# First-norm row sums of two 256-row halves moved from VectorE to ScalarE, with a new instruction order

## The chip, the cores and the metric

One core of a Trainium2 chip runs the kernel. The metric is the device time in microseconds. "The kernel before" and "the changed kernel" are the two sides of the change.

Engines in the profile: PE is TensorE, DVE is VectorE, ACT is ScalarE, POOL is GpSimd, SP is SyncE, which here only issues DMAs. A line of a timeline holds the start in us, the duration in us, the engine, the source line, the operation, output<-input, the shape and the number of instructions in a row; in brackets stands how long the engine was idle just before and what ended that. SPq and ACTq lines are DMA issues.

## The reference

A transformer block in bf16 on x of 1 x 2048 x 512, conditioned on a vector c:

```python
mod = (silu(c) @ w_mod).reshape(1, 6, 1, 512)          # sa, ca, ga, sb, cb, gb
h = layernorm(x) * (1 + ca) + sa
x = x + ga * attention(h, wqkv, wo)    # 32 heads of 16, window of 8 keys, every second position
h = layernorm(x) * (1 + cb) + sb
x = x + gb * ((gelu(h @ w_gate) * (h @ w_up)) @ w_down)  # inner width 1792
```

## The kernel before

The 2048 rows are worked in five groups (g0, g1 of 256 rows, g2 to g4 of 512; a "half" is 256 rows). Python records 1016 operations with their reads and writes; a list `ORDER`, found by a search with a cost model, says in which order they are given out. The program gives each engine its own instructions in that order and sets semaphores between engines. Buffers are rings, used in the order in which their tiles first occur in `ORDER`.

```python
for tag, bufs in (..., ("xn1", 2), ("xn2", 2), ..., ("vR", 2), ("h2T", 2), ("gl", 3), ("ub", 3), ...):
    pool(tag, bufs)
for tag, bufs in (("psF", 4), ("psL", 2), ("psB", 2)):
    pool(tag, bufs, space=PSUM)
...
def ln(g, dst, off, p, seq, tags=("psF", "psF"), sums=None):
    for half in range(n // 256):
        ...
        if sums is not None:        # second norm: the sums came with the residual addition
            nm, var = sums[half], mv
            dve(... tensor_scalar_mul(out=nm[:], in0=nm[:], scalar1=-1.0 / D) ...)
            for i in range(2):
                act(... activation(out=xn[:, i, :], in_=x[g, c0 + i], func=ACT.Square,
                                   bias=nm[:, i:i + 1], accum_out=mv[:, 0, i:i + 1]) ...)
            dve(... rstd = mv / D + 1e-5 ...)
        else:                       # first norm
            for i in range(2):
                dve(... bn_stats(out=st[:, i, :], in_=x[g, c0 + i]) ...)
                dve(... bn_aggr(out=mv[:, i, :], in_=st[:, i, :]) ...)
            dve(... rstd = var + 1e-5 ...)
        gp(... rstd = rstd ** -0.5 ...)
        for i in range(2):
            dve(... xn = (x - mean) * rstd ...)
```

Attention's sums (over the features of each head, and later over the keys; "folds") are narrow matmuls: `tile_position=(0, 32 * d4)`, four 32-column tiles side by side (shape 128*32 in the profile); the others have the shape 128*128. v is written to DRAM (`scr`) and read back in copies that are shifted against each other (`vR`, four parts to a tile), half of them issued from SyncE's queue and half from ScalarE's. The rows of the first norm are transposed by TensorE for g0 to g2 and by a transposing DMA for g3 and g4 (`hT`), those of the second norm by a transposing DMA throughout (`h2T`).

Of the kernel before, what the change touches and what calls it, by code (L numbers as in the profile page):

```python
# [8 lines left out]
ACT = mybir.ActivationFunctionType  # L9
ALU = mybir.AluOpType  # L10
AX = mybir.AxisListType
F32 = mybir.dt.float32
# [6 lines left out]
    56, 7, 0, 55, 1, 4, 8, 9, 40, 42, 41, 33, 5, 6, 13, 137, 43, 16, 138, 44, 139, 10, 34, 45, 35, 36, 267, 140, 46,  # L19
    141, 273, 47, 142, 48, 11, 3, 51, 37, 38, 143, 39, 49, 274, 144, 148, 150, 50, 52, 265, 275, 276, 145, 146, 277,  # L20
    278, 53, 12, 57, 268, 266, 269, 54, 149, 279, 58, 270, 271, 28, 460, 59, 468, 461, 458, 2, 62, 147, 60, 61, 63,
    153, 14, 64, 272, 65, 154, 66, 459, 280, 466, 15, 70, 71, 32, 29, 462, 463, 18, 91, 67, 68, 69, 72, 90, 92, 93,
    467, 687, 281, 282, 283, 159, 160, 285, 284, 697, 161, 286, 288, 162, 17, 287, 94, 95, 96, 97, 98, 99, 469, 470,
    695, 151, 696, 163, 76, 164, 155, 74, 156, 157, 158, 297, 298, 471, 465, 100, 698, 152, 472, 101, 311, 312, 464,
    102, 103, 474, 77, 73, 75, 689, 170, 104, 78, 299, 85, 300, 303, 86, 304, 473, 105, 174, 313, 23, 314, 699, 79,
    173, 80, 305, 306, 690, 688, 172, 106, 691, 107, 108, 109, 293, 294, 309, 310, 291, 292, 171, 692, 110, 475, 476,
    478, 295, 20, 19, 301, 307, 81, 165, 21, 693, 111, 175, 112, 115, 176, 113, 117, 22, 116, 114, 694, 89, 290, 479,
    177, 700, 701, 118, 702, 289, 326, 24, 703, 477, 296, 328, 166, 302, 482, 498, 120, 168, 82, 83, 704, 25, 167,
    119, 123, 121, 124, 122, 308, 490, 178, 179, 481, 483, 169, 84, 180, 125, 499, 486, 127, 496, 491, 497, 494, 487,
    126, 327, 181, 484, 485, 495, 334, 182, 183, 492, 315, 333, 325, 493, 128, 335, 706, 336, 488, 500, 504, 184, 185,  # L30
    480, 329, 705, 708, 707, 129, 131, 330, 331, 332, 337, 501, 338, 339, 320, 340, 719, 130, 132, 489, 186, 341, 342,
    505, 187, 188, 727, 728, 720, 731, 732, 135, 502, 503, 136, 723, 733, 734, 729, 134, 133, 730, 316, 27, 26, 318,
    725, 724, 319, 189, 193, 343, 192, 196, 191, 190, 344, 194, 195, 197, 199, 345, 346, 347, 726, 721, 198, 717, 516,
    519, 722, 217, 219, 518, 227, 216, 520, 348, 317, 517, 718, 525, 349, 521, 522, 350, 351, 524, 526, 322, 523, 324,
    218, 226, 228, 221, 352, 229, 202, 222, 87, 88, 223, 710, 353, 354, 357, 220, 224, 241, 225, 200, 201, 203, 230,
    527, 243, 506, 247, 236, 249, 238, 246, 248, 242, 244, 232, 204, 205, 356, 355, 206, 207, 208, 245, 209, 250, 231,
    233, 234, 237, 715, 360, 361, 363, 239, 528, 529, 530, 358, 359, 716, 531, 533, 210, 321, 30, 31, 235, 323, 364,
    511, 512, 711, 712, 362, 240, 211, 215, 213, 214, 212, 713, 258, 709, 513, 259, 365, 366, 367, 260, 251, 261, 370,
    368, 747, 371, 369, 372, 373, 714, 748, 262, 755, 252, 253, 254, 255, 374, 375, 746, 408, 407, 409, 410, 376, 403,
    263, 405, 377, 382, 383, 418, 508, 420, 402, 404, 384, 515, 745, 256, 380, 514, 378, 381, 385, 386, 411, 379, 532,  # L40
    534, 387, 388, 389, 417, 419, 428, 430, 390, 391, 392, 406, 427, 429, 431, 535, 421, 413, 422, 412, 415, 414, 396,
    264, 507, 536, 257, 393, 394, 395, 432, 424, 416, 433, 435, 434, 754, 753, 537, 538, 423, 425, 444, 437, 438, 397,
    740, 749, 750, 751, 426, 752, 757, 758, 539, 540, 759, 541, 436, 542, 756, 509, 445, 439, 440, 446, 400, 510, 401,
    399, 441, 447, 448, 398, 648, 650, 543, 544, 649, 651, 557, 624, 623, 625, 626, 638, 598, 600, 442, 652, 546, 640,
    599, 659, 603, 639, 627, 545, 549, 550, 661, 558, 561, 760, 601, 605, 562, 564, 658, 553, 602, 660, 555, 455, 556,
    641, 642, 662, 452, 604, 606, 607, 613, 547, 762, 615, 548, 761, 619, 608, 610, 763, 621, 454, 614, 609, 559, 560,
    616, 551, 552, 554, 563, 451, 618, 620, 593, 611, 764, 765, 567, 612, 766, 622, 568, 735, 739, 767, 571, 617, 572,
    741, 736, 569, 633, 635, 595, 570, 580, 634, 565, 566, 743, 738, 453, 768, 769, 636, 582, 581, 573, 594, 596, 597,
    770, 637, 583, 771, 449, 457, 643, 645, 575, 450, 584, 586, 644, 653, 737, 646, 574, 576, 585, 456, 647, 655, 742,
    629, 631, 654, 772, 628, 630, 744, 656, 675, 577, 578, 663, 579, 632, 664, 773, 657, 775, 786, 785, 587, 443, 588,  # L50
    592, 591, 665, 666, 589, 676, 590, 681, 677, 678, 669, 774, 679, 680, 777, 776, 682, 683, 684, 685, 670, 671, 686,
    672, 667, 673, 778, 779, 780, 781, 787, 842, 782, 844, 838, 840, 783, 843, 845, 853, 852, 854, 837, 839, 784, 855,
    788, 790, 789, 792, 856, 791, 846, 793, 872, 832, 834, 794, 795, 796, 797, 857, 841, 874, 859, 858, 860, 833, 861,
    835, 836, 827, 829, 873, 888, 890, 875, 887, 800, 876, 802, 803, 804, 805, 806, 889, 828, 830, 831, 798, 847, 849,
    848, 891, 808, 850, 851, 823, 825, 867, 869, 822, 824, 799, 807, 826, 868, 870, 878, 883, 885, 882, 871, 801, 880,
    674, 668, 816, 809, 811, 810, 884, 886, 863, 877, 879, 865, 862, 864, 881, 866, 892, 812, 813, 814, 910, 911, 904,
    905, 815, 817, 893, 912, 898, 899, 913, 894, 906, 895, 900, 914, 896, 915, 907, 897, 908, 818, 820, 819, 821, 972,
    901, 902, 971, 974, 973, 976, 937, 978, 939, 936, 938, 975, 940, 927, 977, 979, 980, 929, 952, 954, 921, 923, 926,
    928, 922, 924, 925, 931, 951, 953, 955, 930, 933, 916, 941, 918, 943, 942, 944, 932, 934, 945, 935, 917, 919, 920,
    947, 949, 956, 957, 958, 959, 960, 961, 963, 962, 946, 982, 948, 964, 965, 981, 966, 950, 984, 967, 968, 969, 983,  # L60
    903, 909, 970, 986, 987, 988, 985, 989, 992, 993, 994, 995, 996, 997, 990, 991, 998, 999, 1000, 1001, 1004, 1005,
    1006, 1007, 1010, 1011, 1012, 1008, 1002, 1013, 1014, 1009, 1003, 1015,
# [153 lines left out]
def kernel(  # L216
# [13 lines left out]
    nc = tc.nc  # L230
    P = 128
    S, D = 2048, 512
# [9 lines left out]
    PLAIN = 2  # L242
    FIRST = (2, 0, 3, 1)

    pl = Plan(tc)
# [4 lines left out]
    for tag, bufs in (("xs", 4), ("wqkv", 3), ("woP", 1), ("Wg", 2), ("Wu", 2), ("WdP", 1), ("st", 3), ("mv", 4),  # L250
                      ("rstd", 4), ("xsum", 4), ("xn1", 2), ("xn2", 2), ("hT", 2), ("qT", 2), ("kT", 2), ("vT", 2), ("vR", 2), ("prod", 8),
                      ("Lb", 1), ("e", 1), ("rinv", 1), ("rhl", 1), ("oT", 1), ("h2T", 2), ("gl", 3),
                      ("ub", 3), ("hh", 15), ("ot", 2)):
        pool(tag, bufs)
# [10 lines left out]
    T = pl.tile  # L265
    E = Engines(nc, pl)
    pe, act, dve, gp, dma = E.pe, E.act, E.dve, E.pool, E.dma
# [102 lines left out]
    x = Rows()  # L370
# [31 lines left out]
    for b in (1, 0):  # L402
        dma(524e3, lambda dq, b=b: dq.dma_start(
            out=wm01[:, :, b * D:(b + 1) * D], in_=w_mod[:, b * D:(b + 1) * D].rearrange("(t p) n -> p t n", p=P)),
            w=[(wm01, b)], pri=-999.5 + 0.5 * (1 - b), bw=340e3)
# [6 lines left out]
    for d4 in range(4):  # L412
        dma(131e3, lambda dq, d4=d4: dq.dma_start(
            out=woP[32 * d4:32 * d4 + 32, :, :],
            in_=bass.AP(A_wo.tensor, A_wo.offset + 4 * D * d4, [[16 * D, H], [D, 4], [1, D]])), w=[(woP, d4)],
            pri=-987, bw=200e3)
# [77 lines left out]
    def ln(g, dst, off, p, seq, tags=("psF", "psF"), sums=None):  # L494
        n = GROUPS[g][1]
        xns = []
        for half in range(n // 256):
            c0 = 2 * half
            st = T("st", [P, 2, 6], F32, "st", seq)
# [4 lines left out]
            if sums is not None:  # L504
                nm, var = sums[half], mv
                dve(0.09, lambda nm=nm: nc.vector.tensor_scalar_mul(out=nm[:], in0=nm[:], scalar1=-1.0 / D), r=[nm],  # L506
                    w=[nm], pri=p)
# [17 lines left out]
            for i in range(2):  # L525
                def norm(i=i, xn=xn, mv=mv, rstd=rstd, c0=c0, nm=sums and sums[half]):
                    nc.vector.tensor_scalar(
                        out=xn[:, i, :], in0=x[g, c0 + i], scalar1=nm[:, i:i + 1] if nm else mv[:, i, 0:1],
                        scalar2=rstd[:, i:i + 1], op0=ALU.add if nm else ALU.subtract, op1=ALU.mult)

                dve(0.32, norm, r=[x.key(g, c0 + i), mv, rstd] + ([sums[half]] if sums else []), w=[(xn, i)], pri=p)
# [257 lines left out]
    def emit_ffn(g):  # L789
        n = GROUPS[g][1]  # L790
        nf = SG // n
        hh, ends = [], []
# [24 lines left out]
        for c4 in range(n // P):  # L817
# [4 lines left out]
            for part in range(parts):  # L822
# [3 lines left out]
                for lo, hi in ((0, 4), (4, 8), (8, 12), (12, 14)):  # L826
                    def down(lo=lo, hi=hi, c4=c4, y_ps=y_ps, c0=c0, w=w):
# [5 lines left out]
                       w=[y_ps], pri=p, after=ends if parts > 1 else ())  # L833
                ends.append(pl.ops[-1])
# [67 lines left out]
```

## Time and profile before

| | before |
|---|---|
| median of the runs | 243.25 us (242.82 to 243.60, 4 runs in all) |
| first q/k/v matmul | 12.56 us |
| end of the last y matmul | 238.23 us |
| between them, called "the stream" below | 225.67 us |
| ScalarE table loads | 7 |

The stream is what TensorE does without a real pause; what stands before it is the head. A kernel gets slower either because the head slips or because the stream gets longer, so I give both for every run. Each is read from the one execution that was profiled, so differences of a few tenths of a microsecond between two runs are not told from the scatter of executions unless a line of the trace shows where they lie. In the stream of before the profile records one wait of TensorE for another engine, 0.38 us for a gelu at 76.97 us.

### The profile page before, as it was taken

The page shows a single profiled execution, that of the slowest core. Times are in us where ns is not written, and L with a number is a line of the kernel's source. Part 1 is how long each engine was busy: PE and PEld are TensorE (multiplying, and loading weights), DVE is VectorE, ACT ScalarE, POOL GpSimd, SP SyncE. Part 2 cuts the span into 40 slices and gives each one's busy share as a digit, 9 for nine tenths or more (in the row PEclk, how much of TensorE's full clock was granted, in tenths as well). Part 3 has the DMA queues.
Part 4 walks back from the last instruction along what each step waited for, and adds up shares of the span by engine and source line. Part 5 has one row for each costly group of instructions (what it writes and reads, how often), then busy time and mean ns, then how long its engine had stood idle before and what let it go on. Part 6 is the DMA issues. An engine that isn't in the chain of part 4 may idle for free.

```text
span 241.7 us, 4320 instructions
## 1 busy us (share of the span) xinstructions
PE 234.1 (97%) x1664; PEld 128.3 (53%) x1681; DVE 164.1 (68%) x317; ACT 149.5 (62%) x278; POOL 23.3 (10%) x45
## 2 busy tenths in 40 slices
PE   7799999999999999999999999999999999999994
PEld 3499656545677546784444444444444444444443
DVE  4799999998998999775898878873425314131222
ACT  2179889699955763888458894426566542666300
POOL 5548030020000100110000001000010100000000
PEclk9999999999999999999999999999999999999999
DMA  5995899998999150369000837411002022000011
GB/s 178 355 337 159 175 244 307 188 301 209 348 289 252 48 133 3 88 146 210 1 3 0 164 60 175 87 45 44 3 0 45 0 46 87 0 0 0 3 43 43
DMA packets 38970, 29.10 MB, mean 120 GB/s; under 512 B 14117, under 2 KB 38054, under 8 KB 38950
## 3 DMA queue, kind: packets, MB, share of 16 engines
q1 hardware_dynamic: 33424, 24.55, 40.1%
q10 hardware_dynamic: 5526, 4.28, 7.6%
q8 instruction: 13, 0.21, 0.4%
q14 instruction: 7, 0.06, 0.1%
HBM read 21.40 MB, written 4.28 MB: 106 GB/s over the span
## 4 chain that ended last, share of the span: by engine, by line
PE 84%; DVE 6%; DMA 5%; issue 1%; ACT 1%; SPq 0%; POOL 0%; ACTq 0%
PE y_ps L829 20%; PE u_ps L802 18%; PE qkv_ps L604 17%; PE g_ps L802 16%; PE x_ps L779 5%; PE o_ps L764 3%; PE LT L672 3%; DMA vR<-scr 3%; DMA x_sg<-in_A_x_dram 2%; DVE pv L748 2%; DVE WdP L866 1%; DVE st L517 1%; PE LT L702 1%; PE rB L733 1%; DVE hht L814 1%
## 5 line engine op out<-in xcount | busy, mean ns | idle before, releaser
L802 PE MATMUL u_ps<-h2T,Wu 128*128 128x512 bf16 (+1 forms) x280 | 54.5, 336 | 0.4 <-ACT gl L811 0.4
L802 PE MATMUL g_ps<-h2T,Wg 128*128 128x512 bf16 (+1 forms) x280 | 54.9, 337 | 0.0
L829 PE MATMUL y_ps<-WdP,hht 128*128 128x512 bf16 (+1 forms) x231 | 49.2, 366 | 0.5 <-issue 0.2
L811 ACT ACTIVATE gl<-g_ps 128x512 bf16<-128x512 f32 x56 | 32.8, 599 | 24.6 <-PE g_ps L802 18.2
L814 DVE TENSOR_TENSOR hht<-gl,ub 128x512 bf16<-128x512 bf16 x56 | 23.1, 422 | 36.1 <-ACT ub L813 26.3
L604 PE MATMUL qkv_ps<-hT,wqkv 128*128 128x512 bf16 (+1 forms) x230 | 43.6, 339 | 0.2
L813 ACT CAST ub<-u_ps 128x512 bf16<-128x512 f32 x56 | 32.1, 589 | 13.6 <-PE u_ps L802 13.1
L802 PEld LDWEIGHTS <-Wu 128*128 128x128 bf16 x280 | 27.3, 98 | 22.5 <-issue 0.6
L802 PEld LDWEIGHTS <-Wg 128*128 128x128 bf16 x280 | 26.9, 98 | 22.2 <-issue 2.1
L829 PEld LDWEIGHTS <-hht 128*128 128x128 bf16 x238 | 23.1, 98 | 25.3 <-issue 0.7
L523 POOL TENSOR_TENSOR rstd<-rstd,neghalf 128x2 f32<-128x2 f32 x16 | 17.4, 1093 | 167.6 <-DVE rstd L512 152.0
L604 PEld LDWEIGHTS <-wqkv 128*128 128x128 bf16 x232 | 25.0, 114 | 13.9 <-issue 0.8
L748 DVE TENSOR_TENSOR pv<-e,vR 128x2048 bf16<-128x2048 bf16 x24 | 28.4, 1219 | 2.2 <-issue 1.1
L656 DVE TENSOR_TENSOR pq<-qT,kT 128x2048 bf16<-128x2048 bf16 x24 | 28.4, 1221 | 0.2
L539 ACT ACTIVATE h2T<-h2T,modT,scl 128x512 bf16<-128x512 bf16 (+1 forms) x20 | 13.3, 724 | 11.2 <-DMA h2T<-xn 11.2
L843 DVE TENSOR_TENSOR ot<-y_ps,x_sg 128x512 bf16<-128x512 f32 (+1 forms) x13 | 8.2, 647 | 17.3 <-PE y_ps L829 16.0
L779 PE MATMUL x_ps<-woP,oT 128*128 128x512 bf16 x59 | 15.3, 379 | 0.3
L783 DVE SCALAR_TENSOR_TENSOR x_sg<-x_ps,x_sg 128x512 bf16<-128x512 f32 x16 | 10.9, 689 | 5.5 <-PE x_ps L779 5.5
L770 ACT CAST oT<-o_ps 128x512 bf16<-128x512 f32 x16 | 9.2, 600 | 8.1 <-PE o_ps L764 8.1
L509 ACT ACTIVATE xn<-x_sg,xsum 128x512 bf16<-128x512 bf16 x16 | 11.5, 722 | 3.0 <-DVE xsum L506 2.9
L517 DVE BATCH_NORM_STATS2 st<-x_sg 128x6 f32<-128x512 bf16 x16 | 10.5, 679 | 3.6 <-DMA x_sg<-in_A_x_dram 3.6
L620 ACT CAST kT<-qkv_ps 128x512 bf16<-128x512 f32 x16 | 9.3, 590 | 2.1 <-PE qkv_ps L604 2.0
(93 smaller groups left out, 199.6 us busy)
## 6 DMA issues: line engine op xcount, KB each, us to landing
vR<-scr SPq DMA_DIRECT2D x12, 260.0 KB, 4.3
vR<-scr ACTq DMA_DIRECT2D x12, 260.0 KB, 3.8
wm<-in_w_mod_dram SPq DMA_DIRECT2D x6, 512.0 KB, 6.2
out_dram<-ot SPq DMA_DIRECT2D x15, 128.0 KB, 1.7
Wg<-in_B_w_gate_dram SPq DMA_DIRECT2D x2, 896.0 KB, 8.2
Wu<-in_B_w_up_dram SPq DMA_DIRECT2D x2, 896.0 KB, 5.6
WdP<-in_B_w_down_dram SPq DMA_DIRECT2D x2, 896.0 KB, 12.9
scr<-vT SPq DMA_DIRECT2D x6, 264.0 KB, 8.4
```

Source lines behind the costliest of these rows:

```text
L517: dve(0.59, lambda i=i, st=st, c0=c0: nc.vector.bn_stats(out=st[:, i, :], in_=x[g, c0 + i]), r=[x.key(g, c0 + i)], w=[(st, i)], pri=p)
L523: gp(0.7, lambda rstd=rstd: nc.gpsimd.tensor_tensor(out=rstd[:], in0=rstd[:], in1=neghalf[:, 0:2], op=ALU.pow), r=[rstd, neghalf], w=[rstd ...
L539: act(0.29 + n * 0.0008, lambda dt=dt: nc.scalar.activation(out=dst[:, 0:n // P, dt, :], in_=dst[:, 0:n // P, dt, :], func=ACT.Identity, s ...
L604: nc.tensor.matmul(ps[:, j - j0, :], lhsT=wqkv[b][:, dt, j:D:4], rhs=h_cols(hT, g, dt), start=(dt == 0), stop=(dt == DT - 1))
L656: dve(1.14, lambda j=j, wg=wg, t=pq[m]: nc.vector.tensor_tensor(out=t[:], in0=_ap(q[g][:, j, 0:n], [[0, 4], [1, n]]), in1=_ap(k[g][:, j, : ...
L748: dve(1.14, lambda jj=jj, jl=jl, wg=wg, t=pv[m]: nc.vector.tensor_tensor(out=t[:], in0=_ap(e[:, wg, :], [[0, 4], [1, n]]), in1=vR[g][jj][: ...
L779: nc.tensor.matmul(x1_ps[:], lhsT=oT[:, j, c4 * P:(c4 + 1) * P], rhs=woP[:, j, :], start=(j == 0), stop=(j == 3))
L802: nc.tensor.matmul(ps[:, ft - f0, :], lhsT=Wt[ft // 7][:, dt, ft % 7 * P:(ft % 7 + 1) * P], rhs=h_cols(h2, g, dt), start=(dt == 0), stop=( ...
L811: act(0.485, lambda gl=gl, ps=gu[0]: nc.scalar.activation(out=gl[:], in_=ps[:], func=ACT.Gelu_apprx_tanh), r=[gu[0]], w=[gl], pri=p, table ...
L813: act(0.475, lambda ub=ub, ps=gu[1]: nc.scalar.copy(out=ub[:], in_=ps[:]), r=[gu[1]], w=[ub], pri=p)
L814: dve(0.335, lambda gl=gl, ub=ub, ht=ht: nc.vector.tensor_tensor(out=ht[:], in0=gl[:], in1=ub[:], op=ALU.mult), r=[gl, ub], w=[ht], pri=p)
L829: nc.tensor.matmul(y_ps[:], lhsT=hh[ft // nf][:, ft % nf, c4 * P:(c4 + 1) * P], rhs=WdP[:, ft, c0:c0 + w], start=(ft == 0), stop=(ft == FT ...
```

## The change

Its intent: VectorE is busiest in the first 100 us. So for the second group and the first half of the third (g1, and half 0 of g2) the row sums of the first norm are taken on ScalarE, by two passes over the rows with an accumulator (Identity scaled by -1/512 for minus the mean, then Square about it), and the list of the order was searched anew.

```diff
 ORDER = [
-    56, 7, 0, 55, 1, 4, 8, 9, 40, 42, 41, 33, 5, 6, 13, 137, 43, 16, 138, 44, 139, 10, ...
+    5, 8, 7, 1, 0, 6, 9, 40, 42, 41, 43, 44, 45, 47, 46, 13, 137, 3, 138, 139, 33, 34, ...
   (the list of 1016 places is a new one)
+    ACT_STATS = ((1,0),(2,0),)
-  ("xsum", 4)
+  ("xsum", 8)
@@ ln()
+            moved = seq == "ln1" and (g, half) in ACT_STATS
+            if moved:
+                sums = {half: T("xsum", [P, 2], F32, "xsum", "ln1")}
+            elif seq == "ln1":
+                sums = None
...
+                if moved:
+                    for i in range(2):
+                        act(0.75, ... nc.scalar.activation(
+                            out=xn[:, i, :], in_=x[g, c0 + i], func=ACT.Identity, scale=-1.0 / D,
+                            accum_out=nm[:, i:i + 1]) ...)
+                else:
+                    dve(0.09, ... tensor_scalar_mul(out=nm[:], in0=nm[:], scalar1=-1.0 / D) ...)
@@ emit_ffn(g): a list "ends", which only fed the search, is gone
```

## The prediction

> **What bounds the kernel now.** I read the busy table first, then the slices, then the chain of work that ended last, and last the timelines of TensorE (PE), ScalarE (ACT) and VectorE (DVE).
>
> ```profile
> span 241.7 us, 4320 instructions
> ...
> PE 234.1 (97%) x1664; PEld 128.3 (53%) x1681; DVE 164.1 (68%) x317; ACT 149.5 (62%) x278; POOL 23.3 (10%) x45
> ...
> PE   7799999999999999999999999999999999999994
> ...
> DVE  4799999998998999775898878873425314131222
> ACT  2179889699955763888458894426566542666300
> ```
>
> PE is busy in every slice from about 12 us on. DVE is 80% busy or more from 12 to 97 us and slack later; ACT is full in places of that stretch. A busy PE could still be a slow one, so I check its pace in the timeline of PE:
>
> ```profile
> 211.26 3.62 PE L802 MATMUL g_ps<-h2T,Wg 128*128 128x512 bf16 x16
> 214.72 3.62 PE L802 MATMUL u_ps<-h2T,Wu 128*128 128x512 bf16 x16
> ...
> 225.94 12.29 PE L829 MATMUL y_ps<-WdP,hht 128*128 128x512 bf16 x69
> ```
>
> From the start of one group of 16 to the next is 3.46 us: 0.216 us for a 512-wide matmul. In the same way a 256-wide one takes 0.109 us. The real work begins with the first qkv matmul at 12.56 us and ends at 225.94 + 12.29 = 238.2 us: 225.7 us. What must lie in it, by the program's counts: 754 matmuls of 512 (y 210, gate and up 336, qkv 144, output projection 64) x 0.216 = 162.6; 348 of 256 x 0.109 = 37.9; the folds of attention, 192 of 512 and 128 of 256, four side by side, 13.8; small products and transposes 6.6. Sum 220.9 us. Each block of folds costs more than its matmuls:
>
> ```profile
> 159.98 1.05 PE L764 MATMUL o_ps<-pv,F 128*32 128x512 bf16 x16
> 160.96 1.04 PE L802 MATMUL g_ps<-h2T,Wg 128*128 128x512 bf16 x4
> ```
>
> Sixteen folds take 0.98 us where 16/4 x 0.216 is 0.86: 0.12 us for going into the narrow tiling and out again. There are 14 such blocks, 1.7 us. So 222.6 of the 225.7 us are work that the change does not touch; **about 3.1 us (1.3%) is all that a better order can win in the stream**. Ahead of it lie 12.56 us of loading, first norm and modulation columns; behind it 3.5 us of last addition and store.
>
> **What the Trainium skill says.** "ScalarE: Activation LUTs", section "What ACT_TABLE_LOAD costs": every switch to another set of functions costs a load of about 1283 ns, plus about 1380 ns of drain. The trace has the first number exactly (mean 1283 ns, seven loads) but not the second: most loads start right behind the instruction before, and only one has 1.2 us of idle time ahead of it. I count 1.28. "TensorEngine Tiling (Array Packing)", section "Key Properties": a change of tiling mode drains TensorE. The trace agrees, with 0.12 us per block. "SBUF — State Buffer", section "SBUF: two separate sides": VectorE and GpSimd share one port pair under an exclusive lock, so one waits out the other. The trace fits: the GpSimd power on two columns, 0.69 us at best, took 5.00 us when four 128x2048 products ran on VectorE.
>
> **The change part by part.** It has three parts.
>
> (a) The sums. For two halves of 256 rows the first norm's statistics leave DVE. The rows of before:
>
> ```profile
> L509 ACT ACTIVATE xn<-x_sg,xsum 128x512 bf16<-128x512 bf16 x16 | 11.5, 722 | 3.0 <-DVE xsum L506 2.9
> L517 DVE BATCH_NORM_STATS2 st<-x_sg 128x6 f32<-128x512 bf16 x16 | 10.5, 679 | 3.6 <-DMA x_sg<-in_A_x_dram 3.6
> ```
>
> Removed from DVE: four bn_stats (4 x 0.679) and four aggregates (4 x 0.168), 3.4 us busy, some 2.8 us of issue time since they overlap by about 0.1 each. Added to ACT: four Squares, which follow each other every 0.72 us in the timeline (2.9 us), and four Identity passes with a sum; these have no per-row bias, so I take the spacing of a plain ACT pass, about 0.55, plus 0.09 of reading the accumulator: 4 x 0.63 = 2.5. Together 5.4 us.
>
> (b) The tables. The changed program's ACT order has ten table loads, before seven. One is new at the start: ACT's first function is now Identity, so a table is loaded for it, and silu's comes after. Two are new further on, since the exponentials of the third group now come after the first gelus. 3 x 1.28 = 3.9 us. ACT thus gains 9.3 us, some 159 of 242 us: still not the bound over the whole.
>
> (c) The new order. PE has the same products and two fewer fillers. I counted blocks of narrow folds along its new order: 18 where there were 14. 4 x 0.12 = **+0.5 us** on PE, which is the bound. The first FFN matmul comes after 92 instead of 132 of the 512-wide qkv matmuls, 40 x 0.216 = 8.6 us earlier. Dropping the list that made the last column halves wait has no effect at run time: it fed only the search for an order. The last instruction is still a 256-wide y, its addition and its store, so the tail stays.
>
> **The head.** In before, the second half of the modulation columns decides: the weights land at 10.70, and ACT copies modT at 11.29.
>
> ```profile
> 10.70 0.55 PE L463 MATMUL modT_ps<-scT,wm 128*128 128x1 bf16 x16 [0.27 <-DMA wm<-in_w_mod_dram]
> ...
> 11.29 0.16 ACT L470 COPY modT<-modT_ps 128x4 f32<-128x4 f32 x1 [1.33 <-PE modT_ps L463]
> ...
> 12.10 0.41 DVE L561 TENSOR_SCALAR hT<-tp,scl,modT 128x256 bf16<-128x256 bf16 x1
> ```
>
> Walking the new ACT order by these durations: table at 2.74, rows of the second group at 4.3, two Identities to 5.6, two Squares to 7.1, silu table to 8.4, scT to 8.6. The columns can't start before 9.2, when their weights land, so this still fits with 0.5 us to spare. Then two Identities, a Square, scl at about 10.7, the other Square, modT at 11.5 instead of 11.29. On DVE less stands ahead of hT, which in before started only at 12.10, 0.6 us after modT was there. So the first qkv matmul should come at 12.4 to 12.9: **+0.1 us**.
>
> **The middle.** Until 60 us DVE paces the attention products. I walked its new order against PE's from row to row: at the first folds, at the first broadcast of the inverse sums and at the first o folds the two meet within 0.5 us, on either side. The 2.8 us freed on DVE are spent on starting the FFN earlier, not on a shorter PE stream, as PE did not wait for DVE. The narrow place is new: from the third up-projection to the gelus after the exponentials ACT has 14 passes (5 casts of the up-projection, 4 gelus, 2 exponentials, 2 casts of o, a k) of 0.49 us and three table loads of 1.28, 10.7 us together, and PE beside it has 12.2 us of matmuls with four PSUM buffers between them. On average it fits, but three loads make it lumpy, so I put a stall of **+0.4 us** (0 to 1.5) on it. Against that stands up to 3.1 us of waits in before that the new order may partly save; a search for an order would hardly have kept a worse one, by its own reckoning: **-0.4 us**.
>
> Sum: 242.97 + 0.5 + 0.1 + 0.4 - 0.4 = **243.6 us**.
>
> **The rivals.** *The order wins.* DVE is 80% busy or more up to 97 us; if PE's 3.1 us of losses are waits for DVE that the profile hides within pipelined matmuls, freeing 2.8 us of DVE gives most of it back: about 241.5 us. Against it: PE's recorded waits from 13 us on are few, the largest 0.38 us, and that one is for ACT. *ACT becomes the bound* between 50 and 75 us, with table loads and two more passes through each gelu and exponential phase; PE, with four PSUM buffers, waits for every load: up to 3 x 1.28 us, 246 to 247 us. For it: the longest waits of before already name ACT. Against it: PE has qkv work to put between. *The head slips.* If ACT's first loads land late or silu's table drains as the skill says, scT comes at 10, the columns wait, and all later work moves by 1 to 1.5 us: 244.5 us. *Nothing moves*: PE's stream is fixed, 242.5 to 243.5 us.
>
> **Range and chances.** Faster by over 2% would need 4.9 us, more than the 3.1 us that exist in the stream, so only a shorter head could help, and that hangs on the weights: 1%. Slower by over 2% needs two of the bad cases at once: 5%. Within 2%: 94%. Range for eight in ten: 242.2 to 245.4 us.
>
> **What would show it.** Right: the first qkv matmul between 12.4 and 12.9 us; DVE busy down by about 3.4 us, ACT up by 9 to 10, with ten table loads; PE's stream from first qkv to last y 225.5 to 227.5 us; PE's waits after 13 us below 2 us in sum, most of them for ACT between 50 and 75 us. Wrong: scT after 9.2 us with the columns waiting for it; a PE wait above 1 us for DVE products; a stream below 224.5 us, which would mean that DVE did hold PE in before; or a granted clock below 1.

## The result

The changed kernel took 245.05 us (244.95 to 245.76, 4 runs) beside 243.25 us of the kernel before in the same rounds; ratio 1.0081, 95% interval 1.0053 to 1.0109: same within 2%, and slower by some 0.8%, with 1 outside the interval. (A ratio is the mean time of one kernel's fast runs over the mean of the other's in the same rounds, so it is not quite the ratio of the medians.) Executions over 1.5% slower than the fastest of the same kernel are left out of the means.

The busy table and the slices of ScalarE and VectorE of the changed kernel:

```profile
PE 235.2 (97%) x1658; PEld 127.6 (52%) x1679; DVE 162.0 (67%) x309; ACT 158.9 (65%) x297; POOL 24.8 (10%) x45
...
DVE  3589989999999984398989577459633622222222
ACT  4989788879889667975555588705767642666300
```

ScalarE gained 9.4 us, VectorE lost 2.1. TensorE is still busy in all slices. Its timeline at the places that matter:

```profile
12.62 0.60 PE L620 MATMUL qkv_ps<-hT,wqkv 128*128 128x256 bf16 x4
...
39.32 0.40 PE L776 MATMUL o_ps<-pv,F 128*32 128x256 bf16 x8 [0.73 <-DVE pv L766]
...
61.09 1.05 PE L814 MATMUL u_ps<-h2T,Wu 128*128 128x256 bf16 x8 [0.18 <-DMA Wu<-in_B_w_up_dram]
...
227.69 12.29 PE L841 MATMUL y_ps<-WdP,hht 128*128 128x512 bf16 x68
```

The head ends at 12.62 us (before 12.56). The last y matmul ends at 227.69 + 12.29 = 239.98 us, so the stream is 227.36 us: **1.7 us longer, and all of the loss is in the stream**.

In the head, ScalarE's timeline has the two steps that the prediction walked to:

```profile
8.62 0.17 ACT L453 ACTIVATE scT<-c_ps 128x4 bf16<-128x4 f32 x1
...
11.55 0.16 ACT L471 COPY modT<-modT_ps 128x4 f32<-128x4 f32 x1
```

To see where the stream loses, I laid the time from each group's start to the next group's start against what its matmuls need (0.216 us for 512 columns, 0.109 for 256). Over the stream the kernel before loses 4.0 us on that, the changed kernel 5.7. The losses fall in two kinds.

*Turns.* A block of narrow matmuls costs 0.12 us when TensorE comes out of it, as I had seen, **and 0.09 to 0.10 on the full group ahead of it**, which I had not. So 0.21 to 0.22 us per block: 14 blocks are about 3.0 us, 18 blocks 3.8; +0.85.

*Waits.* By the same reckoning, which takes in a little more than the recorded idle times, new are 0.95 us at 37 to 39 us, where the folds wait for a VectorE product, and 0.34 us at 60 to 61 us for the second half of Wu; gone are the 0.55 us that the kernel before loses around its wait for the gelu. The rest, in pieces of under 0.25 us, is 0.6 in the changed kernel and 0.5 in the kernel before. Net +0.84.

Together that is the 1.7 us. The two new waits can be followed back. VectorE's timeline, then SyncE's:

```profile
34.63 4.63 DVE L766 TENSOR_TENSOR pv<-e,vR 128x2048 bf16<-128x2048 bf16 x4 [0.61 <-DMA vR<-scr]
```

```profile
25.39 1.58 SPq L546 DMA_TRANSPOSE hT<-xn  x1
27.07 0.68 SPq L637 DMA_DIRECT2D scr<-vT  x1
27.81 0.63 SPq L641 DMA_DIRECT2D vR<-scr  x1
...
35.91 2.08 SPq L386 DMA_DIRECT2D Wg<-in_B_w_gate_dram  x2
47.55 1.28 SPq L546 DMA_TRANSPOSE h2T<-xn  x1
...
49.50 0.64 SPq L386 DMA_DIRECT2D Wu<-in_B_w_up_dram  x1
```

The last part of g0's vR is issued behind a transposing DMA and a scratch write that had to wait for their data, at 27.81 us, and lands about 34.6. The second half of Wu is issued behind a transposing DMA that waits until 47.55 us, and SyncE does nothing between 38 and 47.5 us. Both look like mere accidents of the issue order. One of them was not, as the runs show.

### The profile page after: what moved, and what is told of

The parts are those of the page before. It is cut to its first block, busy times and chain, and to the rows that moved or that the text cites.

```text
span 243.3 us, 4319 instructions
## 1 busy us (share of the span) xinstructions
PE 235.2 (97%) x1658; PEld 127.6 (52%) x1679; DVE 162.0 (67%) x309; ACT 158.9 (65%) x297; POOL 24.8 (10%) x45
## 4 chain that ended last, share of the span: by engine, by line
PE 83%; DMA 8%; ACT 2%; SPq 2%; issue 1%; DVE 1%; DVEq 0%; ACTq 0%
PE y_ps L841 20%; PE g_ps L814 19%; PE u_ps L814 19%; PE qkv_ps L616 12%; PE x_ps L791 6%; DMA Wu<-in_B_w_up_dram 5%; PE o_ps L776 3%; DMA woP<-in_A_wo_dram 2%; PE LT L684 2%; DMA x_sg<-in_A_x_dram 1%; ACT xn L514 1%; DVE pv L766 1%; ACT xn L521 1%; SPq L414 1%; PE tp L563 1%
## 5 line engine op out<-in xcount | busy, mean ns | idle before, releaser
L814 PE MATMUL u_ps<-h2T,Wu 128*128 128x512 bf16 (+1 forms) x280 | 55.1, 337 | 0.2 <-DMA Wu<-in_B_w_up_dram 0.2
L616 PE MATMUL qkv_ps<-hT,wqkv 128*128 128x512 bf16 (+1 forms) x229 | 44.4, 339 | 0.2
L826 DVE TENSOR_TENSOR hht<-gl,ub 128x512 bf16<-128x512 bf16 x56 | 22.5, 421 | 28.1 <-ACT ub L825 18.6
L521 ACT ACTIVATE xn<-x_sg,xsum 128x512 bf16<-128x512 bf16 x20 | 14.4, 720 | 1.0 <-DVE xsum L518 0.9
L632 ACT CAST vT<-qkv_ps 128x512 bf16<-128x512 f32 x16 | 9.3, 589 | 3.1 <-DMA Wg<-in_B_w_gate_dram 1.5
L632 ACT CAST qT<-qkv_ps 128x512 bf16<-128x512 f32 x16 | 9.4, 594 | 2.6 <-PE qkv_ps L616 2.6
```

The source lines that it names most:

```text
L521: act(0.75, lambda i=i, xn=xn, nm=nm, mv=mv, c0=c0: nc.scalar.activation(out=xn[:, i, :], in_=x[g, c0 + i], func=ACT.Square, bias=nm[:, i: ...
L616: nc.tensor.matmul(ps[:, j - j0, :], lhsT=wqkv[b][:, dt, j:D:4], rhs=h_cols(hT, g, dt), start=(dt == 0), stop=(dt == DT - 1))
L632: act(0.475, lambda t=t, off=off, j0=j0, ps=ps: nc.scalar.copy(out=t[:, j0:j0 + nj, off:off + n], in_=ps[:]), r=[ps], w=[(t, j) for j in r ...
L814: nc.tensor.matmul(ps[:, ft - f0, :], lhsT=Wt[ft // 7][:, dt, ft % 7 * P:(ft % 7 + 1) * P], rhs=h_cols(h2, g, dt), start=(dt == 0), stop=( ...
L826: dve(0.335, lambda gl=gl, ub=ub, ht=ht: nc.vector.tensor_tensor(out=ht[:], in0=gl[:], in1=ub[:], op=ALU.mult), r=[gl, ub], w=[ht], pri=p)
```

## The experiments

`move(a, b)` takes operation a out of `ORDER` and puts it right behind b; it is code that runs ahead of the build and changes nothing else. Each run was timed in five rounds. All results were correct. Nearly all executions have a mean granted clock of 0.997 to 1.0; a few that count as fast have 0.991 to 0.993 and are longer (of the kernel before 244.66 to 245.41 us, beside a median near 243.3). By plain means, leaving out all under 0.997 on both sides raises e2 from 1.0155 to 1.0176 and e4 from 1.0045 to 1.0066, lowers e9 from 1.0193 to 1.0158, and moves the others by 0.001 at most; it reverses no reading below. Line numbers of the source differ from run to run by the lines that an edit adds.

| run | median us | ratio to before, 95% interval | first q/k/v | stream |
|---|---|---|---|---|
| before | 243.25 | 1 | 12.56 | 225.67 |
| changed kernel | 245.05 | 1.0081 (1.0053 to 1.0109) | 12.62 | 227.36 |
| e1_sums_old_order | 245.80 | 1.0100 (1.0057 to 1.0144) | 14.35 | 226.20 |
| e2_new_order_no_sums | 247.55 | 1.0149 (1.0108 to 1.0191) | 14.58 | 228.31 |
| e3_six_more_turns | 244.86 | 1.0051 (1.0011 to 1.0091) | 12.40 | 227.14 |
| e4_values_first | 244.68 | 1.0043 (1.0003 to 1.0083) | 12.63 | 226.54 |
| e5_weights_first | 246.53 | 1.0121 (1.0088 to 1.0154) | 12.59 | 228.82 |
| e6_sums_old_order_head | 243.82 | 1.0007 (0.9974 to 1.0041) | 12.36 | 226.18 |
| e7_no_sums_free_head | 246.45 | 1.0111 (1.0079 to 1.0144) | 13.69 | 227.68 |
| e8_values_and_weights | 246.22 | 1.0108 (1.0078 to 1.0139) | 12.65 | 228.56 |
| e9_all_values_then_weights | 248.07 (fast runs alone) | 1.0174 (1.0113 to 1.0236) | 12.64 | 232.40 |
| e10_squares_twice | 250.63 | 1.0287 (1.0249 to 1.0326) | 12.53 | 233.50 |
| e11_before_product_first | 242.97 | 0.9975 (0.9939 to 1.0010) | 11.95 | 225.20 |
| e12_before_weights_of_mod_first | 244.81 | 1.0060 (1.0035 to 1.0084) | 14.36 | 225.10 |

The theory: the new order costs the time (turns and waits), the move of the sums does not. The main rival: the ScalarE work of the move, 9.4 us, costs it.

### The move and the order, taken apart

**e1: the sums on ScalarE, the order of before.**

```diff
 (changed kernel's code, ORDER of before)
+move(137, 46); move(138, 137); move(139, 138); move(140, 139)   # g1's four passes
+move(35, 140); move(36, 35)                                     # scT, modT products
+move(266, 51); move(265, 266); move(267, 265); move(268, 37)    # g2's four passes
```

> The sums on ScalarE as in the changed kernel, all else in the order of the kernel before (the eight new ScalarE passes stand where the changed kernel has them on that engine). Theory A (the order costs the time, the move itself costs nothing because its ScalarE passes lie ahead of the first q/k/v matmul): ratio to the kernel before 0.997 to 1.003, TensorE from the first q/k/v matmul to the end of the last y matmul 225.7 us within 0.5, ScalarE busy about 157 us, first q/k/v matmul at 12.4 to 12.8. Rival B (the ScalarE work itself, or its table loads, costs the time): ratio about 1.008, the stream about 227.3 us or the first q/k/v matmul at 13.5 or later.

It took 1.0100, which looks like the rival. But the stream was 226.20 us, and the whole loss was in the head, which my own placing had spoiled. ScalarE's timeline:

```profile
10.24 0.63 ACT L531 ACTIVATE xn<-x_sg 128x512 bf16<-128x512 bf16 x1 [1.59 <-PE tp L580]
```

g2's passes write their by-product into the ring buffer of g0's normed rows, so they wait until TensorE has transposed those; in this order TensorE did that behind the modT products. scl, which stands behind these passes, came at 12.33 instead of 9.79 us. The run says nothing on the rival; it was mended as e6.

**e6: the same, with the head mended.**

```diff
 (as e1, but with these moves)
+move(47, 46); move(137, 47); move(138, 137); move(139, 138); move(140, 139)   # g0's two norms together, g1's passes
+move(35, 140); move(48, 35); move(51, 48); move(36, 51)    # g0's transposes ahead of the modT products
+move(266, 51); move(265, 266); move(267, 265); move(268, 37)                  # g2's passes
```

> Again the sums on ScalarE in the order of the kernel before, but with the head mended. In the first try the first q/k/v matmul slipped to 14.35 us, since the second group's sums waited 1.59 us for the first transposes (they share a buffer) and scl came only at 12.33; here TensorE makes the first group's transposes ahead of the first modT products, as the changed kernel does. Theory A (order costs the time; the move costs nothing if the head holds): first q/k/v matmul at 12.4 to 12.9, stream 225.7 to 226.3, ratio to the kernel before 0.998 to 1.003. Rival B (moving the sums costs by itself): ratio 1.006 or more with the head no later than 12.9.

Ratio 1.0007, head 12.36, stream 226.18: as theory A has it. The same ScalarE passes as in the changed kernel, in the old order, cost nothing that the times show (the interval, 0.9974 to 1.0041, leaves room for at most some 1.0 us). (The stream is 0.5 us longer than before, the head 0.2 shorter; the 0.5 lie in three places of 0.1 to 0.3 us.) The timeline of ScalarE in this run shows where they lie, the first and the last of them:

```profile
4.44 0.63 ACT L534 ACTIVATE xn<-x_sg 128x512 bf16<-128x512 bf16 x1 [0.42 <-DMA x_sg<-in_A_x_dram]
...
10.69 0.71 ACT L541 ACTIVATE xn<-x_sg,xsum 128x512 bf16<-128x512 bf16 x1
```

All eight lie between 4.4 and 11.4 us, ahead of the stream, where ScalarE had been idle nearly throughout.

**e2: the new order, the sums back on VectorE.**

```diff
-    ACT_STATS = ((1,0),(2,0),)
+    ACT_STATS = ()
+move(266, 265)                                   # aggregate behind its statistics
```

> The order of the changed kernel with the sums back on VectorE (bn_stats and bn_aggr in the same places of the order). Theory A (order): ratio to the kernel before 1.005 to 1.010, 18 blocks of narrow matmuls, stream 227.3 us within 0.5; VectorE about 165 us busy, ScalarE about 153. Rival B (the move): ratio 0.998 to 1.002, stream about 225.7.

1.0149, worse than either theory had it: the head slipped to 14.58 us, since VectorE now had six statistics in a row between g0's and g1's norms (the text for e7 says eight; six is what the trace has). The rival has no way to explain a loss without the move; but the head blurs the number, so it was mended too.

**e7: the same, with g2's statistics behind the copies of hT.**

```diff
 (ACT_STATS = () as in e2, and)
+move(141, 140); move(142, 141); move(143, 276); move(144, 143)
+move(265, 54); move(266, 265); move(267, 266); move(268, 267)
```

> Again the changed kernel's order with the sums back on VectorE, but with the head mended: in the first try VectorE ran eight bn_stats in a row before the second group's first-norm, hT came 2 us later and the first q/k/v matmul was at 14.58. Here the third group's sums stand behind the copies of hT. Theory A: first q/k/v matmul at 12.3 to 12.9, stream 227.4 to 228.4, ratio 1.006 to 1.011: the new order is slow without the move too. Rival B (the move is what costs): stream 225.7 to 226.3, ratio 0.998 to 1.003.

1.0111, stream 227.68, head still at 13.69, 0.8 us past what I expected: one copy of hT is at 11.11 us, the other stands behind two more statistics at 13.04. So the new order is slow without the move, by 2.0 us in the stream. The four corners, with the mended heads:

| | order of before | new order |
|---|---|---|
| sums on VectorE | 243.25 (1) | 246.45 (1.0111) |
| some sums on ScalarE | 243.82 (1.0007) | 245.05 (1.0081) |

The order costs the time, with the move and without it. Within the new order the kernel with the move has the lower ratio, but the intervals overlap; its trace has a head shorter by 1.07 us, where the move clears VectorE, and a stream shorter by 0.32.

### What a turn costs

**e3: the kernel before, two blocks of 16 folds broken into eight of 4.**

```diff
+move(842, 778); move(838, 779); move(843, 780)   # full groups between the folds of the first block
+move(872, 788); move(832, 790); move(857, 789)   # and of the second
```

> The kernel before, in which the two blocks of 16 narrow o_ps matmuls of the last group (159.98 and 166.24 us) are broken into four each by full matmuls that stood right behind them: the same 32 narrow matmuls, six more turns from full to narrow tiles and back. No new work. Theory A (a turn there and back costs 0.21 us, as the block starts of both traces show): +1.26 us, ratio 1.005 (1.004 to 1.006). With the 0.12 us of my prediction: +0.7, ratio 1.003. Rival (turns are free, the lost time is waits alone): ratio 1.000 within 0.001.

1.0051, stream 227.14: +1.47 us, of which 0.17 is a longer wait for the gelu at 77 us (0.55 us beside 0.38), ahead of the edited place. 1.30 / 6 = 0.22 us for each turn there and back. TensorE's timeline in this run shows both halves of it:

```profile
159.86 0.40 PE L777 MATMUL o_ps<-pv,F 128*32 128x512 bf16 x4
160.19 1.04 PE L815 MATMUL g_ps<-h2T,Wg 128*128 128x512 bf16 x4
161.16 0.40 PE L777 MATMUL o_ps<-pv,F 128*32 128x512 bf16 x4
```

Four folds side by side take 0.33 us from start to start instead of 0.216, and the four full matmuls between two blocks 0.97 instead of 0.86. There is no wait in any of these lines. The rival, that turns are free, falls.

### The two new waits

**e4: the late part of vR issued behind its sister part.**

```diff
+move(73, 75)
```

> The changed kernel with one DMA issue moved: the last of the four parts of vR of the first group is issued on SyncE right behind its sister part, ahead of the transposing DMA of hT and of the scratch write of the second group. Theory A (this late part made VectorE wait 0.61 us for pv and TensorE 0.73 us for VectorE, and nothing behind made up for it): the wait of the first o_ps matmuls at 39.3 us goes, stream 226.5 us (226.2 to 226.9), ratio to the kernel before 1.004 to 1.0055. Rival: TensorE loses the time again at the next wait (hT or the weights), stream 227.2 or more, ratio about 1.008.

As expected: 1.0043, stream 226.54, 0.82 less than the changed kernel. VectorE's product starts without a wait and the folds' wait shrinks from 0.73 to 0.18 us:

```profile
34.17 4.63 DVE L774 TENSOR_TENSOR pv<-e,vR 128x2048 bf16<-128x2048 bf16 x4
```

```profile
38.85 0.40 PE L784 MATMUL o_ps<-pv,F 128*32 128x256 bf16 x8 [0.18 <-DVE pv L774]
```

So this one was an accident of the issue order, and in the stream of this execution nothing behind it ate the gain. The times show less of it: the medians of the two kernels are 0.4 us apart (245.05 and 244.68), and this one's executions fall into two clusters, three at 244.2 to 244.3 (the profiled one among them) and three at 245.1 to 246.1.

**e5: the second half of Wu issued ahead of h2T.**

```diff
+move(27, 26)
```

> The changed kernel with one DMA issue moved: the second half of Wu is issued on SyncE right behind the second half of Wg, ahead of the transposing DMA of h2T, which kept SyncE waiting until 47.6 us. Theory A (the late Wu made TensorE lose 0.34 us at 60 to 61 us, and nothing later makes up for it): the wait of u_ps for Wu goes, stream 227.0 us (226.9 to 227.2), ratio to the kernel before 1.006 to 1.008. Rival (the transfer is bound by the DMA queues or by the tile's last reader, not by its place in the queue): the wait stays, stream 227.4.

Neither came. The wait for Wu is gone, and the stream is 1.5 us **longer** than the changed kernel's. VectorE's timeline, then TensorE's:

```profile
56.81 1.23 DVE L774 TENSOR_TENSOR pv<-e,vR 128x2048 bf16<-128x2048 bf16 x1 [1.89 <-DMA vR<-scr]
```

```profile
62.51 0.38 PE L722 MATMUL LT<-m,NB 128*128 128x512 bf16 x1 [0.78 <-DVE m L717]
63.84 1.06 PE L784 MATMUL o_ps<-pv,F 128*32 128x256 bf16 x32 [0.96 <-DVE pv L774]
```

In the changed kernel the same product started at 54.89 us without a wait. So the place of Wu was no accident: loaded earlier, it holds up g1's vR, VectorE has no slack at 55 us to make that good, and TensorE loses 0.78 + 0.96 us for the 0.34 it got.

**e8: both.**

```diff
+move(73, 75); move(27, 26)
```

> The changed kernel with both DMA issues moved (the late part of vR and the second half of Wu). If the two waits are independent: stream 226.54 - 0.34 = 226.2 us, ratio to the kernel before 1.002 to 1.004; what is then left over the stream of the kernel before, about 0.5 us, is less than the four more turns of TensorE to narrow tiles (4 x 0.22 = 0.9) less its own wait of 0.4 to 0.5. If the second wait takes up what the first gave: stream 226.6 or more.

1.0108, stream 228.56. VectorE waits 2.21 us for g1's vR at 56.6 us (1.89 in e5), so that against e5 the early vR of g0 is worth only 0.3 us.

**e9: both parts of vR first, then Wu.**

```diff
+move(73, 75); move(166, 168); move(27, 26)
```

> The changed kernel with three DMA issues moved on SyncE: the late part of the first group's vR right behind its sister part, the late part of the second group's vR right behind its sister part (both now ahead of the weights), and the second half of Wu behind Wg. Moving Wu alone had made it worse (stream 228.8 instead of 227.36): vR of the second group, issued at 48.81 us, landed only at 56.8 and VectorE waited 1.89 us for it, while it had not waited in the changed kernel. Theory C (Wu's 896 KB in the full DMA queues pushed that vR back): with that vR ahead of the weights VectorE doesn't wait for it, TensorE doesn't wait for Wu, stream 226.2 us (226.0 to 226.5), ratio to the kernel before 1.002 to 1.004. Rival D (VectorE was late for another reason, such as ScalarE's parts of vR or the scratch write): the wait for vR near 55 us stays, stream 228 or more, ratio 1.009 or more.

1.0174, class unclear, as the interval reaches past 1.02: its fast runs scattered from 246.66 to 250.11, and a sixth, 251.26 at a clock of 0.984, is of the slow state. The profiled execution is the one of 250.11, and its stream is 232.40. Theory C's numbers failed and those of D came, but the longest wait was one that I had in neither: for h2T. VectorE still waits for g1's vR, and the landings in the trace tell for which part: SyncE's two, issued at 35.41 and 36.05 us, landed at 45.0 and 46.2, ScalarE's first at 44.7, and the last, which ScalarE issues at 47.91, at 57.9. So the run did not put all of vR first, whatever its label says: one part of four stayed behind on ScalarE's queue, and moving that was not tried. ScalarE's timeline and VectorE's:

```profile
56.52 2.08 ACT L561 ACTIVATE h2T<-h2T,modT,scl 128x256 bf16<-128x256 bf16 x4 [5.42 <-DMA h2T<-xn]
```

```profile
58.10 1.22 DVE L776 TENSOR_TENSOR pv<-e,vR 128x2048 bf16<-128x2048 bf16 x1 [3.57 <-DMA vR<-scr]
```

The DMA view from 34 to 66 us, in 40 slices of 0.8 us (busy tenths of the 16 DMA engines), tells the rest; first the changed kernel, then e5, then e9:

```profile
DMA  9969999999999999105999999999999999999409
```

```profile
DMA  9969999999999999999926999999999997004989
```

```profile
DMA  8999999999999999999992039999999999999300
```

In the changed kernel SyncE's idle stretch from 38 to 47.5 us is no idle stretch of the DMA engines: they work off what was issued, and run nearly dry at about 46.8 us, just before h2T is issued at 47.55. With Wu ahead the backlog lasts to some 50 us, with a part of vR as well to about 51. h2T, issued at much the same time (47.10 to 47.55 us) in all three, made ScalarE wait not at all, 1.00 us and 5.42 us. In e9 h2T landed 9.3 us after its issue, in the changed kernel after 3.3. The Trainium skill, "DMA: Bandwidth & Descriptors", section "Queues, rings and completion order", says that each DMA engine consumes a ring's descriptors in ring order; these three runs agree. SyncE's transfers landed in the order of their issue wherever a landing is recorded. This does not explain why h2T in e9 took some 5 us more after the dip at 51 us; that stays open.

Nor is all of e9's loss made of waits. Here are TensorE's line and the table by stretches of this execution (after the times: busy us of PE, PEld, DVE, ACT and POOL, the granted clock, the share of the DMA engines and GB/s):

```profile
57.17 0.27 PE L824 MATMUL u_ps<-h2T,Wu 128*128 128x256 bf16 x1 [2.91 <-ACT h2T L561]
...
58.60:62.00 3.40, 3.35 (x16) 2.31 (x16) 1.70 (x3) 3.06 (x7) 0.00 (x0) 0.50 1.10 245
```

Right behind TensorE's wait of 2.91 us the granted clock was 0.5 for 3.41 us (58.60 to 62.02), which by my estimate cost half of that, 1.7 of the 3.6 us by which this stream is longer than e5's. No other trace has such a stretch within the stream. Whether the wait brought the lower clock about, no run tests. The executions of e9 with a clock of 0.998 or 1.0 took 246.66 to 248.07 us, those of e5 246.31 to 246.81: e9 is no better than e5, but most of the 3.6 us belongs to the execution that was profiled, and perhaps part of the 5.42 us too.

### Has ScalarE room?

**e10: the Square passes of the second norm done twice.**

```diff
+                    def sq(...):
+                        for _ in range(1 if moved else 2):
+                            r = nc.scalar.activation(out=xn[:, i, :], in_=x[g, c0 + i], func=ACT.Square, ...)
+                        return r
```

> The changed kernel with each of the 16 Square passes of the second norm done twice on ScalarE (same result): 16 x 0.70 us = 11.2 us more work on ScalarE within the stream, three times the two extra table loads of the change plus. Theory A (ScalarE at 65 per cent has slack, TensorE sets the time): what comes is only the later second norm where VectorE or TensorE is close behind it, stream 227.4 to 228.6 us, ratio to the kernel before 1.008 to 1.013, TensorE waits for ScalarE under 1 us in sum. Rival (the 9 us more of ScalarE work in the change are what made it slower): 11 us more make it at least as much slower again, stream 229 us or more, ratio 1.015 or more.

1.0287, stream 233.50: 11.4 us more busy time on ScalarE made the stream 6.1 us longer. I had expected 1.2 at most, so theory A fell here: that ScalarE is busy for 65% of the span does not show that it has room where work is added. The waits of TensorE in this run, its three longest in the stream (total, times, longest, in us):

```profile
PE o_ps L781 <- DVE pv L771: 1.7, 2, 1.0
PE u_ps L819 <- ACT h2T L556: 1.5, 3, 0.7
...
PE y_ps L846 <- ACT gl L828: 0.8, 1, 0.8
```

These passes stand in the second norm, whose result the FFN waits for; the test makes a chain longer as well as an engine fuller, and does not part the two. It also does not save the rival: the move's own passes lie ahead of the stream (e6), and in the changed kernel TensorE has no recorded wait for ScalarE within the stream. The two additional table loads within the stream (2.6 us of ScalarE) belong to the order: e2 and e7, without the move, have them too. What they cost was not tried by itself; the accounting of the 1.7 us leaves some 0.1 to 0.2 us for it.

### A kernel faster than both?

**e11: the kernel before, one product moved.**

```diff
+move(220, 354)
```

> The kernel before with one VectorE instruction moved: the first product gl x ub of the FFN is made ahead of the second of two 128x2048 products pv that stood before it (1.1 us each). In the trace of before the gelu at 76.32 us waited 2.49 us for it, and TensorE 0.38 us for that gelu, its only wait in the stream. If that is the whole of it: stream 225.67 - 0.4 = 225.3 us (225.1 to 225.5), ratio 0.998 to 0.999, too small to tell by the times alone; the wait of u_ps for gl is gone from the trace. Rival: the product comes no earlier since gl and ub come late, or the later pv makes o_ps wait as much: stream 225.6 or more.

0.9975, interval 0.9939 to 1.0010 (by plain means 0.9984 with one execution of before at a clock of 0.993 left out): not told from the kernel before by the times. The trace is clear: the wait of TensorE for the gelu is gone and the stream is 225.20, 0.47 less. Here is TensorE's timeline of before with the wait, then that of this run without:

```profile
76.97 1.91 PE L802 MATMUL u_ps<-h2T,Wu 128*128 128x256 bf16 x16 [0.38 <-ACT gl L811]
```

```profile
75.81 1.91 PE L810 MATMUL u_ps<-h2T,Wu 128*128 128x256 bf16 x16
```

The head was 0.6 us shorter as well, which the edit doesn't touch; the modulation weights landed earlier in this run (its second modT products start at 10.06 us, in before at 10.70), so only the stream's part is the edit's. It has the lowest ratio, ahead of the changed kernel (0.9975 beside 1.0081, intervals apart).

**e12: as e11, with the modulation weights loaded ahead of the third group's x.**

```diff
+move(220, 354)
+move(16, 11)                                        # the load of x behind the two of wm
+move(267, 144); move(273, 267); move(274, 273)      # its statistics behind the first norms
```

> A try at a kernel that beats both: the kernel before with the VectorE product moved (as in the run before this one, ratio 0.9975) and with the head changed: the two 512 KB loads wm for modT are issued ahead of the 512 KB load of the third group's x, which is not needed until later, and the bn_stats that need this x stand behind the first-norms of the first two groups on VectorE. In the profile of before the products waited 1.2 and 0.27 us for wm, which landed at 9.2 and 10.7 us. If wm is bound by what stands ahead of it in the queues, it lands about 1.3 us earlier (512 KB at some 380 GB/s), modT at 10.0 to 10.6 and the first q/k/v matmul at 11.2 to 11.9; stream as in the run before, 225.2 to 225.6; ratio to the kernel before 0.993 to 0.998. Rival: the head is bound by the wqkv load or by the late bn_stats of the third group, the first q/k/v matmul stays at 12.0 or later, or the stream takes up what the head gave: ratio 0.997 to 1.001.

The first half worked as expected: TensorE's timeline has the two groups of modT products at 7.97 and 9.40 us, 1.2 and 1.3 earlier than in before, with no wait for wm:

```profile
9.40 0.55 PE L475 MATMUL modT_ps<-scT,wm 128*128 128x1 bf16 x16
...
14.36 0.60 PE L620 MATMUL qkv_ps<-hT,wqkv 128*128 128x256 bf16 x4
```

Still the first q/k/v matmul came 1.8 us later. VectorE's timeline:

```profile
10.87 1.29 DVE L529 BATCH_NORM_STATS2 st<-x_sg 128x6 f32<-128x512 bf16 x2 [1.98 <-DMA x_sg<-in_A_x_dram]
...
13.88 0.41 DVE L573 TENSOR_SCALAR hT<-tp,scl,modT 128x256 bf16<-128x256 bf16 x1
```

The rival had it: I had left four statistics, whose x now came late, ahead of VectorE's copies of hT. Moved behind those copies as well, they might give a head near 11.3 us by my estimate (modT is copied at 9.99 us, and in before the first q/k/v matmul came 1.27 us after that copy); that was not run.

## Why the prediction was right, and where it was not

The time, 243.6 predicted beside 245.05 measured, lies in its range near the upper end, and the class is right. By its steps:

1. *The bound.* Right. TensorE's stream sets the time, VectorE's saved work does not shorten it (e6: 226.18 us beside 225.67), and the stream of 227.36 us lies in the 225.5 to 227.5 predicted.
2. *The moved work.* Right for ScalarE: +9.4 us beside 9.3 predicted, ten table loads. VectorE lost 2.1 us, not 3.4: of the two numbers in the prediction, the one for issue time (2.8) is the nearer, as the pieces overlap: in the same order VectorE is busy for 165.0 us without the move (e2) and 162.0 with it.
3. *The head, +0.1.* Right: scT at 8.62, scl at 10.77, modT at 11.55 us (8.6, 10.7 and 11.5 predicted), +0.06 in sum. What I had not seen is that the move is what holds the new order's head: without it the head was at 13.69 (e7).
4. *Turns, +0.5.* The mechanism was right, the term mis-sized. A block costs 0.22 us (e3), not 0.12: I had measured only the way out. Four more blocks are +0.85. With that, of the 3.1 us that the prediction left for a better order, 1.3 are turns that it had not counted.
5. *A stall for ScalarE between 50 and 75 us, +0.4.* Wrong in kind. TensorE waited for VectorE at 39 us, which waited for a DMA, and at 61 us for a DMA. "PE's waits after 13 us ... most of them for ACT" names the failed step. e4 shows the first as worth 0.82 us. I had walked VectorE's new order against TensorE's, but not SyncE's, where an issue stood behind two that had to wait.
6. *The order saves, -0.4.* Wrong. "A search for an order would hardly have kept a worse one, by its own reckoning" trusts a cost model; the order it kept is slower by 1.1% without the move (e7) and 0.7% with it (1.0081 over 1.0007).

Two slips had no part in that: 754 x 0.216 is 162.9, not 162.6, and VectorE is not slack after 97 us but 70% busy or more in all slices but one up to 163 us.

Of the 1.45 us that the sum fell short, 0.35 are turns, 0.85 waits (a net +0.85 where I had put +0.4 and -0.4), and 0.3 the kernel before itself, which in the rounds beside the changed kernel took 243.25 and not the 242.97 that the sum starts from. The cost of a turn is shown by e3, that of the first wait by e4's trace (0.82 us; 0.4 by the medians). For Wu's 0.34 us no order was found that saves it without losing more elsewhere.

## What to carry to other kernels

Here, work that moved to an idle engine ahead of the bound stream cost nothing that the times show, and the time saved on an engine that does not hold the stream gained nothing (e6). So ask which order comes with such a move, since here the order decided. Count turns between narrow and full matmul tiles by their two sides, the group before and the group after. When a DMA issuer stands still, look at the DMA engines before filling the gap: in e5 an earlier transfer was paid for by the one behind it, and a search's order may have left room for that one on purpose or by luck. And before reading a long execution, look at its granted clock stretch by stretch, not only at its mean: 0.993 in e9 hid 3.4 us at half clock.

## What the Trainium skill lacked or had wrong

- "TensorEngine Tiling (Array Packing)", section "Key Properties", says that a change of tiling mode drains TensorE, with no figure. Here a turn from full to 32-column tiles and back cost 0.22 us (1.30 us for six), 0.12 of it behind the narrow block and 0.10 in the full group ahead of it.
- "ScalarE: Activation LUTs", section "What ACT_TABLE_LOAD costs", gives a load of about 1283 ns and some 1380 ns of drain. The load agrees to the nanosecond (mean 1283). The drain is not seen: between a Square's accumulator read at 7.12 us (0.19 long) and the load at 7.33 us lie 0.02 us, and scT follows at 8.62, 0.01 us after the load's end.
- "DMA: Bandwidth & Descriptors", section "Queues, rings and completion order", has the order right but gives no figure for what a backlog does to a transposing DMA: here one landed 3.3 us after its issue with the queues nearly dry; with 896 KB more ahead of it (e5) the work behind it began 5.0 us after its issue, and with a 264 KB part as well (e9) it landed after 9.3 us, of which some 5 stay unexplained.
